# A transformer block on one core: sums, `den`, fills and weight loads of the tile loop in another order

## The chip, the core and the metric

The kernel runs on one core of a Trainium2 chip. The metric is the device time of one execution in microseconds (us); a time is given as the median of several runs. The five engines work side by side, each through its own list of instructions in order: PE (TensorE, matrix products), DVE (VectorE), ACT (ScalarE), POOL (GpSimd) and SP (SyncE, which here only issues DMAs). They wait for one another by semaphores.

## The reference

One sequence of 2048 tokens with 512 channels goes through two blocks, both with a residual sum:

```python
x = A_x
h = x + _A_ref(_layernorm(x), A_wqkv, A_w_phi, A_wo)
h2 = h + _B_ref(_layernorm(h), B_w1, B_b1, B_w2, B_b2)
```

`_A_ref` is linear attention with 32 heads of 16 channels. The queries and keys of each head go through a small matrix `w_phi` and two softmaxes, of the logits and of their negatives, side by side: `phi_q` and `phi_k`. With `kv = phi_k^T v` and `z` the sum of `phi_k` over all tokens, the output of a head is `phi_q kv / (phi_q z + 1e-6)`, and `wo` mixes the heads. `_B_ref` is an MLP across tokens: `w2 gelu(w1 layernorm(h)^T + b1) + b2`, with 2048 tokens in, 1792 hidden and 2048 out, shared over the channels. All is float32. Each large product is made of three products of the operands' high and low parts (`mm3`: high by high, high by low, low by high).

## The kernel before

The tokens are cut into `NT` = 16 tiles of 128. The work has four stages.

*Weights and K/V (to L415).* `w_phi` is folded into the query and key weights. Then, tile by tile, K logits (`k_logits`), V (`v_proj`) and the sums of `kv` are made; the products of K and V take turns on PE, in two PSUM banks each (`ps_k`, `ps_v`). In the turns t = 4, 6, 8, 9, 11 and 13 (`Q_AT`) one tile of queries goes along: its product (`q_mm`), its logits (`q_logits`: maximum, minimum and one or two subtractions on DVE), its exponential on ACT (`q_exp`) and the sums of its exponentials (`q_sums`, two reductions on DVE, one for each sign, L215). Here a scheduler of the framework decides how the instructions of PE, DVE, ACT and POOL interleave.

*Transition (L417 to L504).* From here the order on these four engines is the order of the program (a manual schedule); only SP's DMAs are still placed by the scheduler. Two last K tiles, the last V tiles, and `zB` (the sum of `phi_k`, spread over the partitions) are finished. `s_ez(t)` (L441, POOL) multiplies a tile's exponentials by `zB`. `s_den(t)` (L443, DVE, six steps) sums them (L454), combines them with the sums of exponentials and leaves `W[t]` (L462), the factor of each head. `s_pq(t)` (L465, POOL) multiplies the exponentials by `W[t]`. For tiles 0 and 1 `den` works in a PSUM tile of its own (`ps_d`, "dn"). `kvS` (L504, DVE) is `kv` times a mask.

*The loop over tiles (L658 to L697).* Round `it` works on several tiles at once. On PE, in this order: `s_num(it-1)` (L546, `pn`), the transposes `s_tr(it)` (L528, `tr`), in round 0 `s_kv` (L536, two transposes of `kvS`, which ACT copies to `kvB`), one item of `turn` (half a projection of queries, `q_half`, or a fill), `s_wo(it-1)` (`po`, twelve products), then the other items of `turn`. On ACT: the moments of `h(it-2)` (L577 to L579), `oh` (L550, the high part of `pn`), `pht` (L530, two copies of `tr`), an exponential, `hn` and its high part `hs` (L587, L57), and the high parts of MLP weights (`his`, L600). On DVE: logits, `ol` (L555, the low part of `pn`), the sums of a tile, `s_den(it+2)`, `s_h(it-1)` (L571, the residual sum `h`), and the low parts of weights (`flush`, L606). On POOL: `s_pq(it+1)`, `s_rstd(it-2)` (L582 and L583), `s_ez(it+3)`, the low part of `hs` (L58), and the logits' negatives (`negate`).

What ties a round to the one before: `pn` and `po` share one PSUM tile (`ps_n`, one buffer), so `s_num` waits until DVE has read `po` in `s_h`, and `po` until DVE has read `pn` in `ol`. `tr` and `den` share another (`ps_t`, one buffer), so the transposes of a round wait until `den` of the round before has left `W`, and `den` waits until ACT has read `tr`.

A fill is one tile's share of the first product of the MLP: `fill(p)` adds tile `FN[p]` to two PSUM banks of the pair `p` of hidden tiles (six matmuls). `LAG` = 4 lets `fill(0)` take tile `it - 4`; `fill(1)` begins once all logits are made (round 8), with up to two tiles in a round. `Q_TURNS` lists the halves of query projections of rounds 0 to 7. `fill_load` brings the weights of two tiles (one DMA of 256 KB), `his` and `flush` make their high and low parts, in four buffers each (`wf`). `turn` (L648) decides by `it`, `FL` and `FN` when to load.

*The MLP (from L711).* The remaining fills for `p` = 2 to 6, gelu, and the second product in a form with seven products for eight. Here the scheduler orders the instructions again.

Of the kernel before, what the change touches and what calls it, by code (L numbers as in the profile page):

```python
# [11 lines left out]
AF = mybir.ActivationFunctionType  # L12
# [7 lines left out]
NT = S // P  # L20
# [4 lines left out]
Q_AT = (4, 6, 8, 9, 11, 13)  # L25
V_NOT = (0, 1, 11)
Q_TURNS = ((0, 1), (0, 1), (0, 1), (0, 1), (0,), (1,), (0,), (1,))
LAG = 4
WARM = 9
EPS = 1e-5  # L30

# [2 lines left out]
def block_kernel(ctx: ExitStack, tc: tile.TileContext, x, xT, wT, phic, wo, w1, b1, w2, b2,  # L34
                 kvmask, ident_in, out):
    nc = tc.nc
# [12 lines left out]
    r2 = cst.tile([P, NT], F32, name="r2")  # L49
# [42 lines left out]
    ps_d = a1.enter_context(tc.tile_pool(name="ps_d", bufs=1, space=PSUM))  # L92
# [4 lines left out]
    def load_x(t):  # L97
        raw = kk.tile([P, KD, P], F32, name="xraw", bufs=3)
        nc.sync.dma_start(raw, xT[t])
        return raw  # L100

    def load_h(t):
        XH[t] = kk.tile([P, D], F32, name="xh", bufs=3)
        nc.sync.dma_start(XH[t], x[t * P:(t + 1) * P, :])

    def split_x(t, raw):
        X[t] = big.tile([P, 2, KD, P], F32R, name="xs", tag="big")
        split(X[t][:, 0], X[t][:, 1], raw, nc.gpsimd)
# [53 lines left out]
    def turns(*lists):  # L162

        return [ops[i] for i in range(max(map(len, lists))) for ops in lists if i < len(ops)]

    def run(*lists):
        for op in turns(*lists):
            op()
# [11 lines left out]
    def k_logits(t):  # L180
        k_ops(t, proj(t, wkh, wkl, ps_k, "pk_ps"))
        exps(t, PK[t])
# [8 lines left out]
    def k_norm(t, z=True):  # L191
        sk = wk.tile([P, 2 * H], F32, name="sk", bufs=2)
        nc.vector.reduce_sum(sk, heads(PK[t]), axis=AX.X)
        nc.vector.reciprocal(sk, sk)  # L194
        nc.gpsimd.tensor_mul(heads(PK[t]), heads(PK[t]), sk.unsqueeze(2).to_broadcast([P, 2 * H, DH]))  # L195
        if z and t == 0:
            nc.gpsimd.tensor_copy(zacc, PK[t])
        elif z:
            nc.gpsimd.tensor_add(zacc, zacc, PK[t])  # L199

    def kv(t):

        for n in range(4):
            for c in range(4):
                g = n // 2 * 4 + c
                j = 2 * g + n % 2
                nc.tensor.matmul(kvp[32 * c:32 * c + 32, n, :], VS[t][:, 32 * j:32 * j + 32],  # L207
                                 PK[t][:, g, n % 2 * 64:n % 2 * 64 + 64], start=(t == 0 and n == 0),
                                 stop=(t == NT - 1), skip_group_check=True)

    def q_sum(t):

        SQ[t] = sums[:, t]
        e = signs(EQ[t])
        return [lambda c=c: nc.vector.reduce_sum(SQ[t][:, :, 1 - c], e[:, :, c], axis=AX.X) for c in range(2)]  # L215
# [142 lines left out]
    q = {"mm": 0, "logits": 0, "exp": 0, "sum": 0}  # L358

    def q_mm():  # L360
        if q["mm"] < NT:
            PS[q["mm"]] = proj(q["mm"], wqh, wql, ps_q, "pu")
            q["mm"] += 1
# [9 lines left out]
    def q_exp(lag):  # L373
        n = q["exp"]
        if n < min(NT, q["logits"] - len(MN) - lag):
            exps(n, EQ[n])
            q["exp"] += 1

    def q_sums(lag):
        n = q["sum"]  # L380
        if n < min(NT, q["exp"] - lag + NT * (q["exp"] == NT)):
            q["sum"] += 1
            return q_sum(n)
        return []

    def v_kv():

        nonlocal v
        v_proj(v)
        if v % 2 == 0:  # L390
            kv(v - 2)
            kv(v - 1)
        v += 1
# [4 lines left out]
    for t in range(3, NT - 1):  # L398
        if t + 2 < NT:
            raw = load_x(t + 2)  # L400
            load_h(t + 2)
        if t > 3:
            k_logits(t)
        if t > 3 and t not in V_NOT:
            v_kv()
        if t > 0:
            k_norm(t - 1)
        if t + 2 < NT:
            split_x(t + 2, raw)
            stats_x(t + 2)  # L410
        if t in Q_AT:
            q_mm()
            run(q_logits(0))
            q_exp(0)
            run(q_sums(1))  # L415

    ms = ExitStack()  # L417
    ms.enter_context(tc.manual_schedule(engines={ET.PE, ET.DVE, ET.Activation, ET.Pool}))
# [24 lines left out]
    def s_den(t, pool, name):  # L443


        W[t] = az.tile([P, NPR, 2, 2], F32, name="w", bufs=3)
        other = SQ[t]
        at = []

        def first():  # L450
            bank = pool.tile([P, 8, P], F32, name=name)[:, 0] if name == "tr" else pool.tile([P, P], F32, name=name)
            at.extend((bank[:, 0:64].rearrange("p (g c h) -> p g c h", c=2, h=2),
                       bank[:, 64:96].rearrange("p (g h) -> p g h", h=2)))
            nc.vector.reduce_sum(at[0].rearrange("p g c h -> p (g c h)"), heads(EZ[t]), axis=AX.X)  # L454

        return [first,
                lambda: nc.vector.scalar_tensor_tensor(at[0][:, :, 0], other[:, :, 1], 1e-6, at[0][:, :, 0],
                                                       op0=ALU.mult, op1=ALU.add),
                lambda: nc.vector.tensor_mul(at[0], other, at[0]),
                lambda: nc.vector.reduce_sum(at[1], at[0].rearrange("p g c h -> p g h c"), axis=AX.X),  # L460
                lambda: nc.vector.reciprocal(at[1], at[1]),
                lambda: nc.vector.tensor_mul(W[t], other, at[1].unsqueeze(2).to_broadcast([P, NPR, 2, 2]))]  # L462
# [38 lines left out]
    q_mm()  # L501
    kv(NT - 2)
    kv(NT - 1)
    nc.vector.tensor_mul(kvS, kvp, mask.unsqueeze(1).to_broadcast([P, 4, 64]))  # L504


# [6 lines left out]
    ps_t = a2.enter_context(tc.tile_pool(name="ps_t", bufs=1, space=PSUM, reuse_waits="tile"))  # L513
    ps_n = a2.enter_context(tc.tile_pool(name="ps_n", bufs=1, space=PSUM, reuse_waits="tile"))
    HN, HT, PHT, OS, PO, VE = {}, {}, {}, {}, {}, {}
# [16 lines left out]
    def s_kv():  # L532

        pt = banks("pt")[:, 0, 0:2]
        for b in range(2):
            nc.tensor.transpose(pt[:, b, :], kvS[:, 2 * b:2 * b + 2, :].rearrange("p n f -> p (n f)"), ident)  # L536
        nc.scalar.activation(kvB, pt, AF.Copy)
# [15 lines left out]
    def s_ol(t):  # L553
        oh, ol, pn = OS[t]
        return [lambda: nc.vector.tensor_sub(ol, pn, oh)]  # L555
# [24 lines left out]

    def s_rstd(t):
        nc.gpsimd.tensor_tensor(r2[:, t:t + 1], VE[t][:, 0:1], mhalf[:, :1], op=ALU.pow)  # L582
        nc.gpsimd.tensor_mul(VE[t][:, 1:2], VE[t][:, 1:2], r2[:, t:t + 1])  # L583

    def s_hn(t):
        hn = ak.tile([P, D], F32, name="hn")
        nc.scalar.activation(hn, HT[t], AF.Identity, scale=r2[:, t:t + 1], bias=VE[t][:, 1:2])  # L587
        HN[t] = big.tile([P, 2, D], F32R, name="hs", tag="big")
        split(HN[t][:, 0], HN[t][:, 1], hn, nc.gpsimd)
# [6 lines left out]
    def his():  # L596
        while COMING:
            LATER.append(COMING.pop(0))
            _, raw, wh_ = LATER[-1]
            nc.scalar.activation(wh_, raw, AF.Copy)  # L600
# [17 lines left out]
    FN, FL = [0] * (NF // 2), [0] * (NF // 2)  # L618
# [29 lines left out]
    def turn(it):  # L648

        halves = Q_TURNS[it] if it < len(Q_TURNS) else ()  # L650
        n = [FN[0] <= it - LAG and FN[0] < NT, min(2, max(0, it - LAG + 1 - FN[1])) if q["logits"] == NT else 0]
        for p in range(2):
            if it >= LAG - 2 + 2 * p and FL[p] < min(NT, FN[p] + n[p] + 1 + p):
                fill_load(p)
        return ([lambda i=i: q_half(i) for i in halves] + [lambda: fill(0, ps_f)] * n[0]
                + [lambda: fill(1, ps_q)] * n[1])

    for it in range(NT + 3):  # L658
        if it < NT:
            s_x(it)  # L660
        shifted = q["logits"] - len(MN)
        ql = q_logits(0)
        work = turn(it)
        if 0 <= it - 2 < NT:
            s_moments(it - 2)
        if 0 <= it - 1 < NT:
            s_num(it - 1)
        if it < NT:
            s_tr(it)
        if it == 0:  # L670
            s_kv()
        if it + 1 < NT:
            s_pq(it + 1)
        for w in work[:1]:
            w()
        if q["exp"] < shifted:
            q_exp(0)
        if 0 <= it - 2 < NT:
            s_rstd(it - 2)
        if it + 3 < NT:  # L680
            s_ez(it + 3)
        if 0 <= it - 2 < NT:
            s_hn(it - 2)
        negate()
        his()
        sm = q_sums(0) if q["sum"] <= it + 3 else []
        run(ql[:2] + (s_ol(it - 1) if 0 <= it - 1 < NT else []) + ql[2:] + sm[:1])
        run(s_den(it + 2, ps_t, "tr") if it + 2 < NT else [])
        run(sm[1:])
        if 0 <= it - 1 < NT:  # L690
            s_wo(it - 1)
        for w in work[1:]:
            w()
        if 0 <= it - 1 < NT:
            s_h(it - 1)
        flush()
# [104 lines left out]
    for n, (sp, p) in enumerate(STEPS):  # L801
        t = 2 * sp
# [93 lines left out]
```

## Time and profile before

| what | value |
|---|---|
| median of 3 runs | 531.26 us (531.11 to 532.04) |
| the profiled execution | 532.08 us, its span 530.3 us |
| PE clock granted | 0.999 of full speed |
| rounds 0 to 18 of the loop over tiles | from about 143 to 270 us of the span |

The span reaches from the first to the last instruction of the profiled execution; its device time lies a little around it. Times within the span count from its start. A line number in a profile is that of the kernel before, unless it is said otherwise. In a timeline row stand the start, the duration, the engine, the line, the operation, "out<-in", the shapes, the count, and in square brackets how long the engine had been idle and what it then waited for. In a row of groups stand the count, the summed busy time in us, the mean of one in ns, and the idle time ahead. A row of the waits names who waited for whom, the microseconds in total, how often, and the longest. PEld is the loading of weights into PE, which goes beside its products.

### The profile page before, as it was taken

The numbers are of one execution on the slowest core, as the hardware profiler recorded it, in microseconds if no ns is written. First come the engines' busy times: TensorE is split into PE (matmuls) and PEld (weight loads), VectorE is DVE, ScalarE is ACT, GpSimd is POOL, SyncE is SP. The second block draws the span as 40 slices with busy tenths as digits, with TensorE's granted clock in tenths as the row PEclk, the third lists the DMA queues.
The fourth block names the chain that finished last, engine by engine and source line by source line (L and its number), as shares of the span: only waits on it lengthen the run. The fifth ranks groups of instructions, "written<-read, shape, count | busy, mean of one in ns | idle before, by whom it ended". The sixth has DMA issues, their size and how long they took to land.

```text
span 530.3 us, 10156 instructions
## 1 busy us (share of the span) xinstructions
PE 520.0 (98%) x4000; PEld 447.1 (84%) x4000; DVE 381.6 (72%) x680; ACT 272.6 (51%) x460; POOL 231.5 (44%) x190
## 2 busy tenths in 40 slices
PE   8999999999999999999999999999999999999996
PEld 7888888887877777777778888888899999999996
DVE  6893999976889988685235424835758877978774
ACT  6998834525256768666664423525453342342330
POOL 2479699876989999985333000000001101101110
PEclk9999999999999999999999999999999999999999
DMA  8644210013303323433255333543014555545631
GB/s 310 185 132 120 82 40 21 1 40 102 101 21 99 102 80 102 138 101 101 80 160 178 99 101 99 160 114 86 20 41 107 140 152 135 129 134 123 158 79 41
DMA packets 45487, 55.85 MB, mean 105 GB/s; under 512 B 3968, under 2 KB 33024, under 8 KB 45440
## 3 DMA queue, kind: packets, MB, share of 16 engines
q1 hardware_dynamic: 43136, 51.38, 30.9%
q0 software_dynamic: 2016, 3.67, 5.1%
q8 instruction: 31, 0.51, 0.4%
q10 hardware_dynamic: 288, 0.17, 0.1%
q14 instruction: 16, 0.13, 0.1%
HBM read 46.81 MB, written 8.39 MB: 104 GB/s over the span
## 4 chain that ended last, share of the span: by engine, by line
PE 87%; DVE 6%; ACT 4%; issue 2%; POOL 1%; DVEq 0%; ACTq 0%; POOLq 0%
PE py L790 26%; PE pu L62 11%; PE pu L63 11%; PE pu L64 11%; PE pv L63 3%; PE pv L64 3%; PE pv L62 3%; PE pk_ps L62 2%; PE pk_ps L64 2%; PE pk_ps L63 2%; PE po L64 2%; PE po L62 2%; PE po L63 2%; PE kvp L207 2%; PE tr L528 1%
## 5 line engine op out<-in xcount | busy, mean ns | idle before, releaser
L828 POOL DMA_DIRECT2D out<-ot x14 | 12.5, 1001 | 216.1 <-DVE ot L826 216.1
L790 PE MATMUL py<-uf,whi 128*128 128x256 f32 x560 | 96.2, 283 | 0.0
L62 PE MATMUL pu<-hs,whi 128*128 128x512 f32 x224 | 88.4, 394 | 1.1 <-ACT whi L600 1.1
L57 ACT ACTIVATE whi<-wraw 128x1792 fp32r<-128x1792 f32 x28 | 47.7, 1704 | 77.9 <-PE py L790 72.5
L63 PE MATMUL pu<-hs,whi 128*128 128x512 f32 x224 | 87.3, 390 | 0.0
L64 PE MATMUL pu<-hs,wlo 128*128 128x512 f32 x224 | 86.9, 389 | 0.0
L790 PEld LDWEIGHTS py<-uf,whi 128*128 128x128 f32 x560 | 83.3, 192 | 0.0
L606 DVE TENSOR_TENSOR wlo<-wraw,whi 128x512 fp32r<-128x512 f32 x56 | 44.2, 796 | 49.7 <-ACT whi L600 49.5
L790 PE MATMUL py<-uf,wlo 128*128 128x256 f32 x280 | 69.9, 283 | 0.0
L58 DVE TENSOR_TENSOR wlo<-wraw,whi 128x1792 fp32r<-128x1792 f32 x28 | 56.6, 2022 | 16.2 <-ACT whi L57 15.7
L600 ACT ACTIVATE whi<-wraw 128x512 fp32r<-128x512 f32 x56 | 34.6, 625 | 47.9 <-PE pu L63 43.7
L62 PEld LDWEIGHTS pu<-hs,whi 128*128 128x128 f32 x224 | 42.0, 188 | 10.9 <-ACT whi L600 1.8
L790 PEld LDWEIGHTS py<-uf,wlo 128*128 128x128 f32 x280 | 49.7, 192 | 0.0
L64 PEld LDWEIGHTS pu<-hs,wlo 128*128 128x128 f32 x224 | 42.0, 188 | 8.8
L63 PEld LDWEIGHTS pu<-hs,whi 128*128 128x128 f32 x224 | 42.1, 188 | 8.4
L441 POOL TENSOR_TENSOR ez<-eq,zB 128x1024 f32<-128x1024 f32 x16 | 38.5, 2409 | 3.9 <-ACT zB L485 3.9
L790 PE MATMUL py<-un,whi 128*128 128x256 f32 x224 | 38.4, 283 | 0.0
L195 POOL TENSOR_TENSOR pk<-pk,sk 128x1024 f32<-128x1024 f32 x16 | 31.0, 1942 | 9.9 <-DVE sk L194 9.2
L465 POOL TENSOR_TENSOR eq<-eq,w 128x1024 f32<-128x1024 f32 x16 | 32.8, 2052 | 1.7 <-DVE w L462 1.4
L790 PEld LDWEIGHTS py<-un,whi 128*128 128x128 f32 x224 | 33.2, 192 | 0.1
L199 POOL TENSOR_TENSOR zacc<-zacc,pk 128x1024 f32<-128x1024 f32 x13 | 31.3, 2405 | 0.5
L790 PE MATMUL py<-un,wlo 128*128 128x256 f32 x112 | 27.6, 283 | 0.0
(171 smaller groups left out, 1165.3 us busy)
## 6 DMA issues: line engine op xcount, KB each, us to landing
wraw<-in_w SPq DMA_DIRECT2D x112, 256.0 KB, 2.8
xraw<-in_xT SPq DMA_DIRECT2D x16, 256.0 KB, 3.1
xh<-in_x SPq DMA_DIRECT2D x16, 256.0 KB, 2.7
h<-in_x SPq DMA_DIRECT2D x16, 256.0 KB, 2.6
out<-h SPq DMA_DIRECT2D x16, 256.0 KB, 2.0
out<-ot POOLq DMA_DIRECT2D x14, 256.0 KB, 4.3
wraw<-in_wT SPq DMA_DIRECT2D x12, 256.0 KB, 5.1
wo<-in_wo SPq DMA_DIRECT2D x4, 256.0 KB, 4.2
```

What stands on the lines that cost most here:

```text
L57: nc.scalar.activation(hi, src, AF.Copy)
L58: lo_engine.tensor_sub(lo, src, hi)
L62: nc.tensor.matmul(o, ah, bh, start=first, stop=False)
L63: nc.tensor.matmul(o, ah, bl, start=False, stop=False)
L64: nc.tensor.matmul(o, al, bh, start=False, stop=last)
L195: nc.gpsimd.tensor_mul(heads(PK[t]), heads(PK[t]), sk.unsqueeze(2).to_broadcast([P, 2 * H, DH]))
L199: nc.gpsimd.tensor_add(zacc, zacc, PK[t])
L441: nc.gpsimd.tensor_mul(EZ[t], EQ[t], zB)
L465: nc.gpsimd.tensor_mul(heads(EQ[t]), heads(EQ[t]), W[t].rearrange("p g c h -> p (g c h)").unsqueeze(2).to_broadcast([P, 2 * H, DH]))
L600: nc.scalar.activation(wh_, raw, AF.Copy)
L606: LO.append(nc.vector.tensor_sub(wl_, raw, wh_).ins)
L790: nc.tensor.matmul(o, a[x], b[:, y], start=start and i == 0, stop=stop and i == 2, skip_group_check=True)
```

## The change

Six edits, all in the order of the work; what is computed stays the same.

- The sums of a query tile in the K/V stage no longer lag one tile behind (`q_sums(0)`). In the loop, a tile's sums are made in round 0 and then only when `q["sum"] <= it + 2`; with logits in the round both reductions stand ahead of `den`, otherwise one ahead of `ol` and one behind it.
- `s_den(2)` moves from round 0 to the transition, ahead of `kvS`, and works in the "dn" tile; round 0 has no `den`.
- `s_kv` moves behind the first item of `turn` in round 0.
- The product of the mean and `r` (L583) moves from POOL to ACT, ahead of `hn`.
- `LAG` becomes 3: fills take tile `it - 3`, and the loop ends one round earlier (`NT + 2`). The loads of `p = 1` begin in round 7, those of `p = 0` in round 2 as before; in round 16 loads may go two tiles further ahead.
- In rounds after 16 the high parts of weights are made ahead of the moments.

```diff
-LAG = 4
+LAG = 3
...
             q_exp(0)
-            run(q_sums(1))
+            run(q_sums(0))
...
     kv(NT - 1)
+    run(s_den(2, ps_d, "dn"))
     nc.vector.tensor_mul(kvS, kvp, mask.unsqueeze(1).to_broadcast([P, 4, 64]))
...
     def s_rstd(t):
         nc.gpsimd.tensor_tensor(r2[:, t:t + 1], VE[t][:, 0:1], mhalf[:, :1], op=ALU.pow)
-        nc.gpsimd.tensor_mul(VE[t][:, 1:2], VE[t][:, 1:2], r2[:, t:t + 1])
 
     def s_hn(t):
         hn = ak.tile([P, D], F32, name="hn")
+        nc.scalar.activation(VE[t][:, 1:2], VE[t][:, 1:2], AF.Copy, scale=r2[:, t:t + 1])
         nc.scalar.activation(hn, HT[t], AF.Identity, scale=r2[:, t:t + 1], bias=VE[t][:, 1:2])
...
-            if it >= LAG - 2 + 2 * p and FL[p] < min(NT, FN[p] + n[p] + 1 + p):
+            ahead = n[p] + 1 + p + 2 * (it == NT)
+            if it >= (LAG - 1, len(Q_TURNS) - 1)[p] and FL[p] < min(NT, FN[p] + ahead):
                 fill_load(p)
...
-    for it in range(NT + 3):
+    for it in range(NT + 2):
...
         work = turn(it)
+        if it > NT:
+            his()
...
-        if it == 0:
-            s_kv()
         if it + 1 < NT:
             s_pq(it + 1)
         for w in work[:1]:
             w()
+        if it == 0:
+            s_kv()
...
-        sm = q_sums(0) if q["sum"] <= it + 3 else []
-        run(ql[:2] + (s_ol(it - 1) if 0 <= it - 1 < NT else []) + ql[2:] + sm[:1])
-        run(s_den(it + 2, ps_t, "tr") if it + 2 < NT else [])
-        run(sm[1:])
+        sm = q_sums(0) if it == 0 or q["sum"] <= it + 2 else []
+        ol = s_ol(it - 1) if 0 <= it - 1 < NT else []
+        run(ql[:2] + ol + ql[2:] + sm if ql else sm[:1] + ol + sm[1:])
+        if it > 0 and it + 2 < NT:
+            run(s_den(it + 2, ps_t, "tr"))
```

## The prediction

> **What bounds the kernel now.** I read the page first, then who waited for whom on the tensor engine, then busy time in stretches cut where each round's `s_num` starts, then the chain of waits inside one slow round.
>
> ```profile
> span 530.3 us, 10156 instructions
> ```
>
> ```profile
> PE 520.0 (98%) x4000; PEld 447.1 (84%) x4000; DVE 381.6 (72%) x680; ACT 272.6 (51%) x460; POOL 231.5 (44%) x190
> ```
>
> ```profile
> PE pn L546 <- DVE h L571: 2.1, 4, 0.7
> ...
> PE tr L528 <- DVE w L462: 0.6, 1, 0.6
> ```
>
> The tensor engine (PE) is busy for 98% of the span, and the change takes no matrix product away. So the only thing to win is PE's idle time, and these two rows name most of it: 2.1 us in which `s_num` waited for the residual sum `h`, and 0.6 us in which a transpose waited for the weights `W`. Where these lie (window; PE, PEld, DVE, ACT, POOL busy; clock; DMA):
>
> ```profile
> 154.48:161.70 7.22, 6.97 (x74) 5.43 (x74) 6.90 (x15) 5.41 (x11) 6.48 (x7) 1.00 0.26 75
> 161.70:169.47 7.77, 7.11 (x72) 5.35 (x73) 7.60 (x16) 5.14 (x11) 7.61 (x8) 1.00 0.31 101
> 169.47:177.03 7.56, 6.98 (x72) 5.43 (x73) 6.66 (x15) 5.67 (x12) 7.40 (x8) 1.00 0.23 72
> 177.03:184.00 6.97, 6.97 (x72) 5.42 (x73) 6.29 (x13) 5.79 (x12) 6.89 (x6) 1.00 0.36 116
> 184.00:191.93 7.93, 7.28 (x73) 5.35 (x73) 7.62 (x15) 5.25 (x11) 7.77 (x8) 1.00 0.31 98
> ...
> 259.70:270.00 10.30, 9.27 (x69) 6.98 (x68) 2.08 (x5) 6.57 (x15) 3.19 (x6) 1.00 0.32 102
> 270.00:385.00 115.00, 114.92 (x508) 95.05 (x509) 59.41 (x112) 50.00 (x90) 7.76 (x9) 1.00 0.38 113
> ```
>
> Rounds 2 to 6 of the loop over tiles, then the loop's end, then the MLP. Round 5 shows what a round costs when PE never waits: 6.97 us. Rounds 2, 3, 4 and 6 take 0.25, 0.80, 0.59 and 0.96 more: idle of 0.25, 0.66, 0.58 and 0.65, and a slower pace of 0.14 in round 3 and 0.31 in round 6. After 270 PE is full again, so whatever is won before 270 reaches the end. Why a round is long, from the chain of waits:
>
> ```profile
> 169.59 0.82 ACT hj L578 x2
> ...
> 172.54 0.59 DVE smq L215
> 173.14 1.14 DVE tr L454
> ...
> 176.20 0.70 DVE h L571 x2
> ```
>
> It is a ring: `h` lets ScalarE (ACT) take the moments, ACT's order puts `oh` behind them, VectorE (DVE) needs `oh` for `ol`, then works through shift, sums (L215) and `den` (its first reduction is L454) to the next `h`, which frees the bank for `s_num`. From the moments' second step (169.59) to the end of the next `h` (176.20 + 0.62) it is 7.23 us; with the first step of 0.20 (its row stands below) and the hand-over from `h` to ACT the ring is some 7.5 us, more than PE's 6.97. That DVE shows idle time in these rounds is no contradiction: it waits for `oh` while ACT does the moments, and both are links of the same ring.
>
> **The change, part by part.**
>
> *Sums (L415, L686).* By the order of the built program, no sums stand in rounds 1 to 4; tile 5's pair moves to the K/V stage, tile 6's to round 0, and tiles 7 to 15 follow one round later than before (rounds 5 to 13), ahead of `den`.
>
> ```profile
> L215 DVE TENSOR_REDUCE smq<-eq 128x32 f32<-128x512 f32 x32 | 21.2, 674 | 0.2 <-ACT eq L171 0.2
> ```
>
> A sum lasts 0.67 us, of which the next instruction overlaps a little: it advances DVE by 0.60 (172.54 to 173.14), a pair by 1.2. In rounds 2, 3 and 4 the ring shrinks from some 7.5 to 6.3, under 6.97: their idle (0.25, 0.66, 0.58) goes, with about 0.6 to spare. What is late next there is PE itself. In round 5 there are no logits, so one sum runs in the gap in which DVE waits for `oh`, and the ring stays under 6.97. Round 6 keeps logits and both sums ahead of `den`; no weight part precedes it now, and round 5 leaves it the lead of about 0.6, so of its 0.65 I let 0.2 stand. Saved: 0.25 + 0.66 + 0.58 + 0.45 = 1.94. Of the slower pace (0.14 + 0.31 = 0.45), matmuls that started one by one behind late operands, I take half, 0.25; bounds 0 and 0.45.
>
> *The third tile's `den` ahead of `kvS`; `s_kv` behind the first half projection.*
>
> ```profile
> 139.20 2.40 POOL L441 TENSOR_TENSOR ez<-eq,zB 128x1024 f32<-128x1024 f32 x1
> ```
>
> ```profile
> 143.26 0.42 DVE L504 TENSOR_TENSOR kvS<-kvp,mask 128x256 f32<-128x256 f32 x1 [1.31 <-PE kvp L207]
> ```
>
> ```profile
> 145.40 1.22 DVE L454 TENSOR_REDUCE tr<-ez 128x64 f32<-128x1024 f32 x1
> ...
> 147.81 0.22 DVE L462 TENSOR_TENSOR w<-smq,tr 128x64 f32<-128x64 f32 x1
> ```
>
> ```profile
> 148.18 0.71 PE L528 MATMUL tr<-ident,eq 64*128 64x64 f32 x16 [0.60 <-DVE w L462]
> ```
>
> DVE is idle from 141.95 (143.26 less 1.31). Tile 2's `ez` is ready at 141.60, so `den(2)` starts at 141.95 and ends after 2.63 us (145.40 to 148.03) at 144.58, 3.4 earlier. It also uses another PSUM tile, so round 1's transposes don't wait: 0.60 saved. Queued behind it on DVE is `kvS`, on which `s_kv`, `kvB` and the first `s_num` hang; `kvS` slips to about 145.0. The stretch from 270 shows the pace of a full PE, 115.00 us for 508 matmuls or 0.227 each, so the half projection of six that now stands ahead of `s_kv` takes 1.37. PE ends `kvp` at about 143.2, transposes for 0.7 and reaches `s_kv` at about 145.2, cover 0.2; without it PE would wait at most 1.2. After 144.58 DVE has `kvS` (0.4), three steps of logits (1.8), the pair of sums (1.2), two steps of the next logits (1.2) and `ol(0)` (0.6), so `ol(0)` ends at 149.8. PE, its transposes now at 147.58, wants it 0.7 + 1.37 later, at 149.6: I charge 0.2.
>
> *`VE*r` on ACT.*
>
> ```profile
> L577 ACT ACTIVATE ve<-ve 128x1 f32<-128x1 f32 x16 | 3.2, 203 | 28.2 <-DVE h L571 28.2
> ```
>
> ```profile
> L583 POOL TENSOR_TENSOR ve<-ve,r 128x1 f32<-128x1 f32 x16 | 3.1, 192 | 1.2
> ```
>
> The first row is an ACT operation of the new one's shape, the second the POOL operation that goes. POOL loses 0.19, ACT gains 0.20 per tile. ACT is busy 5.1 to 5.8 us in these rounds and it stands behind `oh` and `pht`; it waits for POOL's `r` just as `hn` did, with `hn`, `hs` and the weights' high parts queued behind it, so it only makes the fills' operand some 0.2 later. Cost nothing, hidden by the slack worked out under the first rival.
>
> *Fills three behind, weight loads at other times.* PE gets no more work: one fill of 1.37 goes into round 3, the loop loses its last round. `p = 1` loads from round 7 instead of 4, `p = 0` in even rounds. Each load is a DMA on SP's queue, which stands in the built order several `h` loads ahead of its conversion; the ACT and DVE conversions number four in rounds 2 to 7 as before. Zero here.
>
> *The last weights.* Before, `p = 0`'s last pair came in round 17 and was converted behind tile 15's `hs`:
>
> ```profile
> 269.41 1.66 ACT L600 ACTIVATE whi<-wraw 128x512 fp32r<-128x512 f32 x3
> ```
>
> ```profile
> 270.08 0.50 PE L62 MATMUL pu<-hs,whi 128*128 128x512 f32 x1 [1.11 <-ACT whi L600]
> ```
>
> ```profile
> 264.98 0.69 DVE L571 SCALAR_TENSOR_TENSOR h<-po,h 128x512 f32<-128x512 f32 x1 [3.18 <-PE po L64]
> ```
>
> ```profile
> 269.58 1.28 POOL L58 TENSOR_TENSOR hs<-hn,hs 128x512 fp32r<-128x512 f32 x1 [1.59 <-ACT hs L57]
> ```
>
> With a lag of 3 the parity puts that load in round 16, converted behind tile 14's `hs`, some 6 us earlier than 269.4: the 1.06 (1.03 by the window, 1.11 by the row) goes. What is late next is tile 15's operand: 5.9 us from its `h` to 270.86. The built order puts 42 matmuls, 9.6 us, between `po(15)` and the first use of it (tile 13's half, tile 14 and four tiles of `p = 2`), so it is covered by over 3 us.
>
> Sum: 0.60 - 0.20 + 1.94 + 0.25 + 1.06 = **3.65 us saved**. The profiled execution took 532.08 around its span of 530.3, so by its own time 528.4; the median of the three runs is 531.26, which gives **527.6**.
>
> **Rivals.**
>
> *POOL takes over.* POOL is as busy as DVE in these rounds, and its low parts now have one round less before a fill wants them.
>
> ```profile
> 148.11 1.94 POOL L465 TENSOR_TENSOR eq<-eq,w 128x1024 f32<-128x1024 f32 x1 [0.91 <-DVE w L462]
> ...
> 177.72 2.39 POOL L465 TENSOR_TENSOR eq<-eq,w 128x1024 f32<-128x1024 f32 x1
> ```
>
> ```profile
> 197.56 1.30 POOL L58 TENSOR_TENSOR hs<-hn,hs 128x512 fp32r<-128x512 f32 x1
> ```
>
> ```profile
> 200.14 0.50 PE L62 MATMUL pu<-hs,whi 128*128 128x512 f32 x1
> ```
>
> ```profile
> 176.81 1.50 DVE L606 TENSOR_TENSOR wlo<-wraw,whi 128x512 fp32r<-128x512 f32 x1
> ```
>
> Tile 5's low part ends at 198.86; round 8's first fill, which will want tile 5, stood at 200.14: 1.3 of slack. PE comes 2.6 earlier, less 1.37 for the extra fill; POOL gains the 0.91 for which it waits for `W(2)`, and 0.19 in each of five rounds: slack 1.3 - 1.2 + 1.9 = 2.0. It decides if POOL is more than 2.0 late, for example because `eq` takes 2.39 instead of 1.94 in every round up to there, 3.2 in all: then some 1.2 to 1.5 of the gain is lost, 529.1.
> The Trainium skill (SBUF — State Buffer, Who interferes with whom) says that a VectorE instruction with two SBUF inputs and a GpSimd one that reads SBUF exclude each other fully, and that reductions never do. By that rule the moved sums cost POOL nothing, and only the four `wlo` do; the trace agrees in kind (1.50 beside 2.39), though both were stretched, neither blocked for the other's length.
>
> *Slower: sums crowd the K logits.* Without the lag of one, a turn's sums wait for that turn's own exponential and stand ahead of K's logits in DVE's order. If K's banks then came free too late, each of the six turns would cost PE a pair, 1.2 us: 7.2 - 3.65, so 534.8. It decides once a bank's slack is under 1.2; here it is 4.9 (the bank of the `K` read last at 88.28 is wanted at 93.22):
>
> ```profile
> 87.61 0.67 DVE L149 TENSOR_TENSOR pk<-mn,pk_ps 128x512 f32<-128x512 f32 x1
> ```
>
> ```profile
> 93.22 0.39 PE L62 MATMUL pk_ps<-wkh,xs 128*128 128x512 f32 x1
> ```
>
> *It doesn't do what it says.* The early `his()` finds nothing to convert in round 17, since no load is left by then; if the load of round 16 lands late, only the 1.06 is missing: 528.7.
>
> **Chances.** Forecast 0.70 (own range 526.9 to 528.4), POOL 0.10 (529.1), last weights 0.07 (528.7), gains cancelled by something unseen 0.05 (531), K logits 0.08 (534.8). Faster by over 0.2%, about what a measurement of this kernel tells from no change: 0.87; within: 0.05; slower: 0.08. The range goes from all idle and all slow pace removed (2.1 + 0.6 + 1.1 + 0.45 = 4.25, with half a microsecond for spread) to the POOL case with a little more: 526.5 to 529.6.
>
> **What would show it.** Right: `pn <- h` falls from 2.1 to about 0.2, `tr <- w` and `pu <- whi` vanish, rounds 2 to 7 take 6.97 each (8.34 in round 3), and 270 on stays full. Wrong: fills that wait for `hs` (POOL), `pt` or `po` that waits for DVE in round 0 or 1 by over 0.4, idle PE between 60 and 143, or waits for `whi` after the loop.

## The result and the profile after

| | median (runs) | lowest to highest |
|---|---|---|
| before | 531.61 us (4) | 531.11 to 532.04 |
| after | 528.53 us (4) | 527.96 to 529.15 |

The ratio after / before is 0.9943, with a 95% interval of 0.9925 to 0.9960: 3.1 us less, or 0.57%. The forecast was 527.6, with its own range of 526.9 to 528.4 and a whole range to 529.6. It started from a median of 531.26 for the kernel before; from 531.61 the same 3.65 saved would give 528.0, so 0.35 of the miss of 0.9 is the starting point. Two executions far off all the others, one of the kernel before (1032.76 us) and one of b_sums (1805.23 us), are left out of the ratios. The profiled execution of the changed kernel took 528.31 us (span 526.5).

The page of the changed kernel, busy time by engine:

```profile
PE 518.9 (99%) x4000; PEld 446.6 (85%) x4000; DVE 386.2 (73%) x680; ACT 278.2 (53%) x476; POOL 229.1 (44%) x174
```

Who waited for whom on PE, in the changed kernel (total, times, longest). Its line numbers are up to 5 above those of before: L547 is `pn`, L556 `ol`, L572 `h`, L607 `wlo`.

```profile
PE po L62 <- DVE ol L556: 1.0, 1, 1.0
...
PE pn L547 <- DVE h L572: 0.2, 1, 0.2
```

`tr <- w` and `pu <- whi` are gone, and `pn <- h` fell from 2.1 to 0.2, as forecast. The first row is new. Rounds 2 to 6 of the changed kernel, cut as those of before:

```profile
153.46:160.35 6.89, 6.89 (x73) 5.39 (x72) 6.20 (x13) 6.07 (x13) 5.40 (x5) 1.00 0.26 78
160.35:168.64 8.29, 8.29 (x79) 6.53 (x78) 7.02 (x15) 6.50 (x14) 8.13 (x8) 1.00 0.39 128
168.64:175.54 6.90, 6.90 (x73) 5.40 (x72) 4.95 (x12) 5.34 (x10) 6.90 (x6) 1.00 0.10 38
175.54:182.47 6.93, 6.93 (x74) 5.40 (x73) 5.74 (x14) 5.68 (x12) 6.85 (x6) 1.00 0.33 111
182.47:189.65 7.18, 6.97 (x73) 5.43 (x73) 6.25 (x15) 5.82 (x12) 7.10 (x7) 1.00 0.20 56
```

PE is full in all but the last, where 0.21 is left of 0.65. Round 3 (8.29) holds one more fill, as announced. Now both kernels over longer stretches: rounds 0 and 1, rounds 2 to 6, rounds 7 to 15, and from there to the first product of the second MLP layer. Before:

```profile
143.12:154.48 11.36, 10.76 (x109) 8.35 (x103) 10.07 (x22) 4.51 (x9) 10.30 (x9) 1.00 0.17 58
154.48:191.93 37.45, 35.31 (x361) 26.97 (x361) 35.06 (x70) 27.26 (x53) 36.16 (x33) 1.00 0.29 92
191.93:259.68 67.75, 67.75 (x672) 53.14 (x673) 47.25 (x95) 46.51 (x96) 53.10 (x46) 1.00 0.33 103
259.68:270.04 10.36, 9.29 (x69) 7.00 (x68) 2.10 (x5) 6.63 (x15) 3.23 (x6) 1.00 0.31 101
270.04:384.58 114.54, 114.50 (x504) 94.63 (x505) 59.23 (x111) 49.54 (x88) 7.72 (x9) 1.00 0.38 113
```

After:

```profile
142.61:153.46 10.85, 10.85 (x110) 8.25 (x103) 9.98 (x23) 4.61 (x9) 10.67 (x9) 1.00 0.20 63
153.46:189.65 36.19, 35.98 (x367) 28.15 (x367) 30.16 (x64) 29.40 (x58) 34.39 (x28) 1.00 0.26 84
189.65:260.13 70.48, 69.44 (x679) 54.07 (x679) 55.95 (x99) 49.98 (x106) 52.50 (x37) 1.00 0.34 108
260.13:268.00 7.87, 7.87 (x64) 6.13 (x64) 2.90 (x7) 5.88 (x14) 1.84 (x2) 1.00 0.31 102
268.00:380.80 112.80, 112.80 (x499) 93.39 (x498) 57.12 (x109) 50.19 (x89) 8.70 (x10) 1.00 0.39 115
```

One fill (1.37) moved into the second stretch and one into the third, out of the last two. With that taken out, the four parts gain 0.51, 2.63 (37.45 - 36.19 + 1.37), -1.36 (67.75 - 70.48 + 1.37) and 1.49 (124.90 - 120.67 - 2.74): 3.27 in all, of which 2.60 is idle time and 0.67 is pace. I call the length from the first transpose of the loop to the first product of the second layer the **loop length**: 241.46 before, 238.19 after. It is the measure for the experiments, because the rest of the 3.8 us between the two profiled executions, 0.51, lies elsewhere, at the very start:

```profile
10.70 2.13 PE L124 MATMUL pk_ps<-wkh,xs 128*128 128x512 f32 x8 [0.80 <-ACT wkh L279]
```

```profile
10.17 2.13 PE L124 MATMUL pk_ps<-wkh,xs 128*128 128x512 f32 x8 [0.80 <-ACT wkh L279]
```

The first K product begins 0.53 earlier in the execution after (second row) than in the one before, in code that the diff does not touch: ACT takes up the second block of weights at 6.32 instead of 6.60, and where the rest of the 0.53 comes from was not traced. In the twelve kernels below this start lies anywhere from 9.94 to 11.09, and from it to the first transpose it is 132.4 or 132.5 us in every one: so much for the K/V stage, which the sums do not disturb at all.

**Where 1.04 us was lost.** DVE and POOL of the changed kernel at the turn from round 8 to round 9, then PE:

```profile
203.50 0.68 DVE L572 SCALAR_TENSOR_TENSOR h<-po,h 128x512 f32<-128x512 f32 x1
...
204.11 3.53 DVE L607 TENSOR_TENSOR wlo<-wraw,whi 128x512 fp32r<-128x512 f32 x2
207.57 0.67 DVE L215 TENSOR_REDUCE smq<-eq 128x32 f32<-128x512 f32 x1
208.16 0.68 DVE L556 TENSOR_TENSOR ol<-pn,oh 128x512 fp32r<-128x512 f32 x1
```

```profile
203.45 1.30 POOL L58 TENSOR_TENSOR hs<-hn,hs 128x512 fp32r<-128x512 f32 x1
204.71 2.39 POOL L465 TENSOR_TENSOR eq<-eq,w 128x1024 f32<-128x1024 f32 x1
207.06 1.00 POOL L583 TENSOR_TENSOR r<-ve,mhalf 128x1 f32<-128x1 f32 x1
```

```profile
208.90 0.50 PE L62 MATMUL po<-woh,oh 128*128 128x512 f32 x1 [1.04 <-DVE ol L556]
```

Both `p = 0` and `p = 1` load in round 8, so two low parts follow `h(7)`. They last 3.53 us instead of some 1.3. POOL's rows tell why, if the two engines cannot read at once: the first part waits for the end of `hs` (204.75), runs for 0.45, and `eq`, 1.94 elsewhere, is held up by just that (2.39). The second part waits for the end of `eq` (207.10) and holds up `r` by 0.45 (1.00 instead of 0.55). Then a sum stands ahead of `ol`, for another 0.60, and `po(8)` waits.

### The profile page after: what moved, and what is told of

The parts are those of the page before. It is cut to its first block, busy times and chain, and to the rows that moved or that the text cites. A ratio compares the mean times of both kernels' runs of the same rounds, so it can differ in the third digit from the quotient of the medians.

```text
span 526.5 us, 10155 instructions
## 1 busy us (share of the span) xinstructions
PE 518.9 (99%) x4000; PEld 446.6 (85%) x4000; DVE 386.2 (73%) x680; ACT 278.2 (53%) x476; POOL 229.1 (44%) x174
## 4 chain that ended last, share of the span: by engine, by line
PE 95%; DVE 3%; ACT 1%; issue 0%; DVEq 0%
PE py L795 26%; PE pu L62 13%; PE pu L63 12%; PE pu L64 12%; PE pv L63 3%; PE pv L64 3%; PE po L62 3%; PE pv L62 3%; PE po L64 3%; PE po L63 3%; PE pk_ps L62 2%; PE pk_ps L64 2%; PE pk_ps L63 2%; PE pn L547 2%; PE tr L529 2%; PE kvp L207 2%
## 5 line engine op out<-in xcount | busy, mean ns | idle before, releaser
L607 DVE TENSOR_TENSOR wlo<-wraw,whi 128x512 fp32r<-128x512 f32 x56 | 48.5, 872 | 44.6 <-ACT whi L601 44.4
L58 POOL TENSOR_TENSOR hs<-hn,hs 128x512 fp32r<-128x512 f32 x16 | 20.7, 1293 | 17.9 <-ACT hs L57 17.9
```

Source lines behind the costliest of these rows:

```text
L58: lo_engine.tensor_sub(lo, src, hi)
L607: LO.append(nc.vector.tensor_sub(wl_, raw, wh_).ins)
```

## The experiments

All but two start from the changed kernel. The loop length is from each one's profiled execution, the ratio from timed runs beside the kernel before. The intervals of u_sums, b_lag, u_kv, fix_ol, fix_load, u_pow and best overlap that of the change, so by time alone they can't be told from it; how they differ from it is read from the loop length and the rows of one trace each.

**Put back the sums (u_sums).**

```diff
-            run(q_sums(0))
+            run(q_sums(1))
...
-        sm = q_sums(0) if it == 0 or q["sum"] <= it + 2 else []
-        ol = s_ol(it - 1) if 0 <= it - 1 < NT else []
-        run(ql[:2] + ol + ql[2:] + sm if ql else sm[:1] + ol + sm[1:])
+        sm = q_sums(0) if q["sum"] <= it + 3 else []
+        run(ql[:2] + (s_ol(it - 1) if 0 <= it - 1 < NT else []) + ql[2:] + sm[:1])
...
             run(s_den(it + 2, ps_t, "tr"))
+        run(sm[1:])
```

> The changed kernel with the sums alone put back: the lag of one in the K/V stage, tile 5's pair in round 0 and so on one round earlier, one reduction ahead of den and one behind it. Theory A (the sums made the ring of h, moments, oh, ol, den too long): PE's waits of pn for h come back in rounds 2, 3, 4 and 6, from 0.2 to about 2.1 us; the 1.04 us in which po(8) waited for ol shrinks to about 0.4, because ol stands ahead of the sums again; time 528.5 + 1.9 + 0.4 - 0.6, about 530.2. Rival (the ring became short for another reason, the earlier den(2) or the third fill in round 3): pn waits for h stay under 0.5 us and the time stays within 0.5 of 528.5.

Measured: 528.65 us, ratio 0.9944 (0.9929 to 0.9959), the same as the change itself; loop length 238.37, 0.18 more.

```profile
PE pn L547 <- DVE h L572: 1.0, 3, 0.5
...
PE po L62 <- DVE ol L556: 0.2, 1, 0.2
```

The time is the rival's, the waits are neither side's. Those for `h` come back only by half, 0.22, 0.21 and 0.55 at the ends of rounds 2, 4 and 6 and none in round 3, and against them stands the 1.04 of `po(8)`, which goes altogether. So my theory that the sums carried the gain fell: among the other edits they are worth 0.2 us. `ol(8)` is not earlier, though:

```profile
208.67 0.68 DVE L556 TENSOR_TENSOR ol<-pn,oh 128x512 fp32r<-128x512 f32 x1
```

```profile
209.41 0.50 PE L62 MATMUL po<-woh,oh 128*128 128x512 f32 x1
```

Counted from the first transpose of the loop (142.91 here, 142.61 in the changed kernel), `ol(8)` ends at 66.44 here and at 66.23 there, and `po(8)` starts at 66.50 and at 66.29. It is PE that comes later here: in the changed kernel it stood ready 1.04 earlier, at 65.25. So up to that point the sums bring PE 1.25 us forward, and the wait for `ol` takes 1.04 of it back. No run puts the sums back where that wait is gone.

**Put back the fills and loads (u_lag).**

```diff
-LAG = 3
+LAG = 4
...
-            ahead = n[p] + 1 + p + 2 * (it == NT)
-            if it >= (LAG - 1, len(Q_TURNS) - 1)[p] and FL[p] < min(NT, FN[p] + ahead):
+            if it >= LAG - 2 + 2 * p and FL[p] < min(NT, FN[p] + n[p] + 1 + p):
...
-    for it in range(NT + 2):
+    for it in range(NT + 3):
...
-        if it > NT:
-            his()
```

> The changed kernel with the fills four tiles behind, the weight loads at the rounds of the kernel before and no early high parts. Theory A (the 1.04 us of po(8) came from two weight loads in round 8, whose low parts took 3.53 us of DVE ahead of ol): the wait of po(8) goes, since p = 1 then starts in round 4 and only one load falls in round 8; the wait of pu for whi in the last round comes back with 1.1 us; time 528.5 - 1.04 + 1.1, about 528.6, with up to 0.6 more where round 3 loses its fill. Rival B (it is the sum ahead of ol alone): po(8) still waits 0.6 or more, and the time is about 529.5.

Measured: 530.79 us, ratio 0.9983 (0.9973 to 0.9992); loop length 240.66, 2.47 more.

```profile
PE po L62 <- DVE ol L556: 1.2, 1, 1.2
PE pu L62 <- ACT whi L601: 1.2, 1, 1.2
...
PE pn L547 <- DVE h L572: 0.7, 1, 0.7
```

The wait of `po(8)` went and that for `whi` came back, as theory A had it; the time is 1.6 us above the most it allowed. The first row is another one: `po(5)`, at 185.65, followed by 0.66 at the end of round 6. ACT, then DVE, ahead of it:

```profile
179.68 0.29 ACT L587 ACTIVATE ve<-ve,r 128x1 f32<-128x1 f32 x1 [1.26 <-POOL r L583]
```

```profile
182.04 1.76 DVE L607 TENSOR_TENSOR wlo<-wraw,whi 128x512 fp32r<-128x512 f32 x1 [1.06 <-ACT whi L601]
```

POOL is late with `r`, ACT waits 1.26 for it with the high part of a weight behind, and DVE waits 1.06 for that. I read it so: with fills four behind round 3 has no fill and lasts 6.9 us, in which POOL, with some 6.9 us of its own, catches nothing up; the fill in round 3 gives POOL and DVE 1.4 us in which PE works. This run puts back two things at once, though, the fills and a low part in round 5. fix_load below parts them: it has low parts in rounds 2, 4 and 5 as this run has, but keeps the fill in round 3, and there `pn` waits the same 0.66 and `po(5)` not at all. So the 0.66 goes with the low part in round 5, and the 1.23 with the missing fill.

**Each of the two alone, on the kernel before (b_lag, b_sums).** First the fills and loads:

```diff
-LAG = 4
+LAG = 3
...
-            if it >= LAG - 2 + 2 * p and FL[p] < min(NT, FN[p] + n[p] + 1 + p):
+            ahead = n[p] + 1 + p + 2 * (it == NT)
+            if it >= (LAG - 1, len(Q_TURNS) - 1)[p] and FL[p] < min(NT, FN[p] + ahead):
...
-    for it in range(NT + 3):
+    for it in range(NT + 2):
...
+        if it > NT:
+            his()
```

> The kernel before with only the fills three behind, the loads of the change and the early high parts. Prediction's terms: only the 1.06 us of the last weights, so 530.5. Theory formed after the run with the sums put back: the fill that moves into round 3 gives POOL and DVE 1.4 us there in which PE works, so most waits of pn for h go as well (2.1 to about 1.0); time 531.6 - 1.1 - 1.1, about 529.4.

Measured: 529.10 us, ratio 0.9955 (0.9943 to 0.9968); loop length 239.19, 2.27 less than before. Its waits:

```profile
PE pn L546 <- DVE h L571: 1.1, 3, 0.6
...
PE tr L528 <- DVE w L462: 0.6, 1, 0.6
PE po L62 <- DVE ol L555: 0.5, 1, 0.5
```

As the later theory had it: `pn <- h` falls from 2.1 to 1.1 with no sum moved. It is the fill that does it and not the loads: up to round 4 the low parts stand in the same rounds as before (2 and 4), and just there the wait at the end of round 3 goes from 0.66 to nothing and that at the end of round 4 from 0.58 to 0.21. Round 6, ahead of which a low part goes as well, keeps 0.59 of 0.66. Then the sums, with `den(2)` left in round 0:

```diff
-            run(q_sums(1))
+            run(q_sums(0))
...
-        sm = q_sums(0) if q["sum"] <= it + 3 else []
-        run(ql[:2] + (s_ol(it - 1) if 0 <= it - 1 < NT else []) + ql[2:] + sm[:1])
+        sm = q_sums(0) if it == 0 or q["sum"] <= it + 2 else []
+        ol = s_ol(it - 1) if 0 <= it - 1 < NT else []
+        run(ql[:2] + ol + ql[2:] + sm if ql else sm[:1] + ol + sm[1:])
...
-        run(sm[1:])
```

> The kernel before with only the sums edit (no lag in the K/V stage, later in the loop, both ahead of den with logits). Prediction's terms: 1.94 + 0.25 us saved, less 1.1 because round 0's pair now stands ahead of den(2), so about 530.5. Theory formed after the other runs: with fills four behind the rounds stay at 7 us, in which POOL is full, and waits of po(5) for ol (1.2) and of pn(6) for h (0.7) take the place of those removed, tr waits 1.7 instead of 0.6, whi stays at 1.1; idle 4.7 against 3.85 before, so 531.6 + 0.5 to 0.9, about 532.3: by itself this edit gains nothing.

Measured: 532.91 us, ratio 1.0016 (1.0006 to 1.0026); loop length 241.10, 0.36 less. Its waits:

```profile
PE tr L528 <- DVE w L462: 1.8, 1, 1.8
PE pu L62 <- ACT whi L600: 1.1, 1, 1.1
...
PE pn L546 <- DVE h L571: 0.6, 1, 0.6
PE po L62 <- DVE ol L555: 0.5, 1, 0.5
```

The idle of the loop is 4.0, against 3.85 before and 4.7 as the later theory had it: of the waits for `h` only the 0.64 at the end of round 6 is left, and waits of another kind have taken the place of the others, 1.2 of them because the pair of sums in round 0 stands ahead of `den(2)`. The time is longer than the loop says; the last section has a likely reason. Alone the sums gain nothing in time.

**Put back `den(2)` (u_den), put back `s_kv` (u_kv).**

```diff
-    run(s_den(2, ps_d, "dn"))
...
-        if it > 0 and it + 2 < NT:
+        if it + 2 < NT:
             run(s_den(it + 2, ps_t, "tr"))
```

> The changed kernel with den(2) alone put back into round 0, in the tr tile, behind the logits and the pair of sums. Theory A: DVE then reaches den(2) after kvS (142.7), three steps of logits (1.8) and the pair of sums (1.2), W(2) is there at about 148.7, and round 1's transposes, wanted at about 147.0, wait for it some 1.7 us, more than the 0.6 of the kernel before; time 528.5 + 1.7, about 530.2. Rival (the wait is 0.6 as before, so that the sums in round 0 cost nothing there): 529.1. Rival 2 (den(2) in the transition only pushes kvS, and putting it back costs nothing): 528.5.

Measured: 530.23 us, ratio 0.9982 (0.9970 to 0.9994); loop length 241.36.

```profile
148.75 0.87 PE L528 MATMUL tr<-ident,eq 64*128 64x64 f32 x16 [1.73 <-DVE w L462]
```

The wait is 1.73, as theory A worked it out. So this edit is what pays for the pair of sums in round 0. The loop is 3.2 longer rather than 1.7; the rest is PE's clock (last section).

```diff
+        if it == 0:
+            s_kv()
         if it + 1 < NT:
             s_pq(it + 1)
         for w in work[:1]:
             w()
-        if it == 0:
-            s_kv()
```

> The changed kernel with s_kv back ahead of the first half projection of round 0. The prediction: without that cover PE waits at most 1.2 us. In the trace of the changed kernel kvS ends at 144.33 and PE would reach s_kv at 143.25, so theory A: PE waits about 1.1 us for kvS, time about 529.6. Rival (kvB on ACT, not kvS, is what the first s_num needs, and it has room): the wait is only moved and the time stays at 528.5.

Measured: 529.38 us, ratio 0.9955 (0.9940 to 0.9969); loop length 239.12, 0.93 more.

```profile
144.35 0.44 PE L537 MATMUL pt<-ident,kvS 128*128 128x128 f32 x2 [1.05 <-DVE kvS L505]
```

Theory A: the half projection ahead of `s_kv` hides 1.05 us.

**The lost 1.04: `ol` first (fix_ol), other rounds for the loads (fix_load), POOL's operation left out (no_pq).**

```diff
-        run(ql[:2] + ol + ql[2:] + sm if ql else sm[:1] + ol + sm[1:])
+        run(ql[:2] + ol + ql[2:] + sm if ql else ol + sm if it > 8 else sm[:1] + ol + sm[1:])
```

> The changed kernel with ol ahead of both sums in rounds 9 to 13 (before: one sum ahead of ol), nothing else. Theory A (two stretched low parts AND the sum stood ahead of ol): the sum is 0.60 of the 1.04 us, so po(8) still waits about 0.4 us; time about 527.9. Rival B (the sum ahead of ol is all of it): no wait is left, time about 527.3. Rival C (den, now 0.6 later behind both sums, makes the next h late): new waits of pn for h in rounds 10 to 13, time 528.5 or more.

Measured: 528.13 us, ratio 0.9933 (0.9918 to 0.9948); loop length 237.60, 0.59 less.

```profile
PE po L62 <- DVE ol L556: 0.4, 1, 0.4
```

0.4 of the 1.04 is left (0.45 in its row of the timeline): theory A. b_lag says the same from the other side: it has the two loads and not the sum ahead of `ol`, and its `po(8)` waits 0.47.

```diff
-            if it >= (LAG - 1, len(Q_TURNS) - 1)[p] and FL[p] < min(NT, FN[p] + ahead):
+            ahead += 2 * (p == 1 and it == 7)
+            if it >= (LAG - 1, 5)[p] and (p, it) != (1, 8) and FL[p] < min(NT, FN[p] + ahead):
```

> The changed kernel with the second load of p = 1 in round 7 and its first in round 5, none in round 8, so that one low part instead of two follows h in round 8; the order of sums and ol is untouched. Theory A (two loads in one round): DVE is 1.7 us earlier at ol(8), po(8) doesn't wait, time about 527.3. Rival B (the sum ahead of ol alone): po(8) still waits some 0.6 us, time about 528.1. Rival C (the parts moved to rounds 5 and 7 lengthen the ring there): pn waits for h in rounds 6 and 8 grow from 0.2 to 0.7 or more, time 528.5.

Measured: 528.09 us, ratio 0.9932 (0.9917 to 0.9947); loop length 237.52, 0.67 less.

```profile
PE pn L547 <- DVE h L572: 0.7, 1, 0.7
```

No wait of `po` is left, with the sum still ahead of `ol`: rival B falls, and theory A has the wait right. Its time of 527.3 isn't reached, because rival C is right for round 6: the part that moved to round 5 raises the wait at its end from 0.21 to 0.66. At the end of round 8, where C had another one, there is none. So both the two loads and the sum are needed for the 1.04: without the sum 0.45 of it is left, without the second load nothing.

```diff
-        if it + 1 < NT:
+        if it + 1 < NT and it != 9:
             s_pq(it + 1)
```

> The changed kernel without the multiplication of tile 10's exponentials by W on POOL in round 9 (the work is left out, one POOL operation of 2.4 us). It asks whether POOL is what stretches the two low parts on DVE at 204 (3.53 us for two, 0.69 each elsewhere). Theory A: without it the two take 1.4 to 2.2 us, po(8) doesn't wait, time about 527.3. Rival B (ez and the low part of hs on POOL, which then stand there instead, stretch them as much, or the stretch has another cause): they take 3 us or more, po(8) waits as before, time 528.5.

Measured: 527.07 us, ratio 0.9911 (0.9898 to 0.9925); loop length 236.86; no wait of `po`. The two parts:

```profile
203.87 1.77 DVE L607 TENSOR_TENSOR wlo<-wraw,whi 128x512 fp32r<-128x512 f32 x2
```

1.77 instead of 3.53 with one POOL operation less: theory A. It is POOL that makes them long.

**POOL's room: `VE*r` back on POOL (u_pow), a tiny power more in rounds 2 to 7 (pool_x).**

```diff
         nc.gpsimd.tensor_tensor(r2[:, t:t + 1], VE[t][:, 0:1], mhalf[:, :1], op=ALU.pow)
+        nc.gpsimd.tensor_mul(VE[t][:, 1:2], VE[t][:, 1:2], r2[:, t:t + 1])
...
-        nc.scalar.activation(VE[t][:, 1:2], VE[t][:, 1:2], AF.Copy, scale=r2[:, t:t + 1])
```

> The changed kernel with the product of mean and r back on POOL. The prediction: worth nothing. In the trace of the changed kernel POOL has no idle time from 160 to 197 and the low part of tile 5 ends 0.9 us ahead of the first fill of round 8 (196.91 against 197.82). Theory A: five products of 0.19 make POOL 0.95 later there, just about the slack, so PE waits 0 to 0.2 us, time 528.5 to 528.7. Rival (POOL is the bound, the rival of the prediction): PE waits 0.5 us or more for hs, time 529.1 or more.

Measured: 528.27 us, ratio 0.9933 (0.9918 to 0.9948); loop length 237.91, 0.28 less. PE doesn't wait for `hs`, and the 1.04 of `po(8)` is gone; in its place `po(10)` waits 0.33. DVE, then POOL, at the same turn:

```profile
204.50 2.52 DVE L607 TENSOR_TENSOR wlo<-wraw,whi 128x512 fp32r<-128x512 f32 x2 [0.51 <-ACT whi L601]
```

```profile
204.74 1.74 POOL L58 TENSOR_TENSOR hs<-hn,hs 128x512 fp32r<-128x512 f32 x1
206.44 2.38 POOL L465 TENSOR_TENSOR eq<-eq,w 128x1024 f32<-128x1024 f32 x1
```

None had foreseen this. DVE now starts 0.24 ahead of `hs` instead of behind it, so the first part runs at once and `hs` is held up by 0.45 (1.74 instead of 1.28); the second waits for `hs` alone. Who is first decides over a microsecond.

```diff
             s_ez(it + 3)
+        if 2 <= it < 8:
+            pj = ak.tile([P, 1], F32, name="pj", bufs=1)
+            nc.gpsimd.tensor_tensor(pj, VE[it - 2][:, 0:1], mhalf[:, :1], op=ALU.pow)
```

> The changed kernel with one more tiny power on POOL in each of rounds 2 to 7 (0.55 us each, its result unused), behind ez. It measures how much room POOL has. Theory A (slack 0.9 us at the first fill of round 8): by round 8 POOL is some 2.7 us later, so PE waits for hs there in sum 1.5 to 2.2 us, and the time is 530.0 to 530.7. Rival (POOL has the 2.0 us of slack that the prediction worked out): waits of 0.5 to 1.0, time 529.0 to 529.5. Rival 2 (POOL is far from mattering): no wait, 528.5.

Measured: 530.44 us, ratio 0.9979 (0.9967 to 0.9991); loop length 239.98, 1.79 more. PE, DVE and POOL:

```profile
PE po L62 <- DVE ol L556: 2.2, 2, 1.8
```

```profile
205.52 4.13 DVE L607 TENSOR_TENSOR wlo<-wraw,whi 128x512 fp32r<-128x512 f32 x2 [0.54 <-ACT whi L601]
```

```profile
205.45 1.30 POOL L58 TENSOR_TENSOR hs<-hn,hs 128x512 fp32r<-128x512 f32 x1
206.69 2.40 POOL L465 TENSOR_TENSOR eq<-eq,w 128x1024 f32<-128x1024 f32 x1
```

The price is theory A's, the place is not: PE waits for `ol`, not for `hs`. DVE came 0.07 behind the start of `hs` and waited for all of it, then for all of `eq`: 1.23 + 0.45 + 1.94 + 0.5 = 4.1.

**All together (best).** fix_load, fix_ol, and tile 7's sums in round 4, where DVE waits 1.4 us for `oh`:

```diff
-        sm = q_sums(0) if it == 0 or q["sum"] <= it + 2 else []
+        sm = q_sums(0) if it == 0 or q["sum"] <= it + 2 + (it in (4, 5)) else []
...
-        run(ql[:2] + ol + ql[2:] + sm if ql else sm[:1] + ol + sm[1:])
+        run(ql[:2] + sm + ol + ql[2:] if it == 4 else ql[:2] + ol + ql[2:] + sm if ql else ol + sm if it > 8 else sm[:1] + ol + sm[1:])
```

> The changed kernel with three edits: the loads of p = 1 in rounds 5 and 7 and none in round 8; ol ahead of both sums from round 9 on; tile 7's sums in round 4 in the gap ahead of ol, tile 8's in round 5, none in round 6. From the earlier runs: the wait of po(8) goes with the loads (seen), and the 0.66 us in which pn waited for h at round 7 goes because round 6 then has no sums, 1.2 us less. Theory: no wait of PE in the tile loop of 0.2 us or more, from the first transpose to the first py 236.6 to 237.0 us instead of 238.2, time 527.0. Rival (DVE's room is used up: each edit moves the wait to the next round): a wait of 0.4 us or more in rounds 4 to 8, time 527.8 or more.

Measured: 528.00 us, ratio 0.9930 (0.9918 to 0.9943); loop length 237.24. The view of the waits lists two rows, both from the first eleven microseconds:

```profile
PE pk_ps L287 <- DVE eps L53: 1.1, 1, 1.1
PE pk_ps L124 <- ACT wkh L279: 0.8, 1, 0.8
```

The waits went as the theory had it; the time did not, 528.0 where it had 527.0 and the rival 527.8 or more. The loop is 0.95 shorter than that of the change, less than the 1.2 to 1.6 expected and less than the 1.25 of idle that is gone; the gain over the change, 0.5 us by the medians, is inside both intervals, so by time alone it isn't shown. This profiled execution had a late start, its first K product at 10.82.

## Why the prediction was right, and where its steps were not

- *`tr <- w`, 0.60 saved:* right. *`po(0)`, 0.20 charged:* nothing was lost; `kvS` ended at 144.33 where I had 145.0 (0.5 of it by the early start), and PE waited neither for it nor for `ol(0)`. u_den and u_kv bear out the working: without the one edit PE waits 1.73, without the other 1.05.
- *Sums, 1.94 saved in rounds 2 to 6:* 2.14 of idle became 0.21, the size of the forecast. For rounds 2 to 4 the ring as I worked it out holds: in b_sums and u_lag, with the sums moved and the fills four behind, no wait for `h` is left there. But in both the wait comes back in round 6, where `po(5)` waits 0.48 and 1.23. **"Fills three behind, weight loads at other times ... Zero here" is what failed.** I counted the fill in round 3 as work moved, not as 1.37 us in which DVE and POOL catch up while PE is busy. It keeps `po(5)` from waiting, and with no sum moved at all it takes away the wait at the end of round 3 and most of that of round 4 (b_lag). The end of round 6 needs both the sums and the load moved out of round 5, which I had booked under the sums ("no weight part precedes it now"): without the sums 0.55 and 0.59 are left (u_sums, b_lag), without the load's move 0.66 (u_lag, fix_load). So that the size came out is partly luck: the sums were credited with what the fills and loads gave.
- *Pace, 0.25 taken:* 0.70 in rounds 2 to 6, above my bound of 0.45. A full round took 6.90 in the changed kernel where I read 6.97 from before.
- *Loads at other times, zero:* also wrong, on the other side: round 8's two loads cost 1.04 of idle, together with the sum ahead of `ol`. In the same stretch 0.32 of pace was lost, whose cause is not shown. I had asked whether each load lands in time and whether as many conversions remain in rounds 2 to 7, but not what stands behind the conversions on DVE in round 9, where the sums edit had just put a reduction ahead of `ol`.
- *`VE*r` on ACT, zero:* undone, the loop is 0.28 shorter (0.57 less idle, 0.29 more busy time on PE), too little for the timed runs to show. What changes the idle time is the moment at which POOL and DVE meet.
- *Last weights, 1.06 saved:* right (1.11), and tile 15's operand was covered.
- *Rivals:* K's logits were not crowded; the K/V stage kept its 132.4 us. POOL didn't take over through late fills, as I had put it, but POOL is close: pool_x shows it acting through `wlo` and `ol`. The last weights came in time: no wait for `whi` is left.

By the four stretches the forecast was 0.40, 2.19, 0 and 1.06 us saved; found were 0.51, 2.63, -1.36 and 1.49. Three were too small and one missed a loss, so 3.65 and 3.27 (3.1 in the medians) lie closer than their terms. That too is luck.

The prediction's sentence on the Trainium skill (SBUF — State Buffer, Who interferes with whom) has to be taken back in part. I wrote that both sides were stretched and neither blocked for the other's length. The rule says that the one that starts first holds the port for its whole instruction, and the rows above agree: each POOL operation that meets a `wlo` is longer by 0.45 (1.94 to 2.39, 1.28 to 1.74, 0.55 to 1.00), and each `wlo` is longer by what was left of the POOL operation. The waiting stands inside the durations, which is why I took it for a slower pace.

## What to carry to other kernels

Work that moves on the bound engine is not free of effect because it is the same work: where it goes, the other engines get time, and where it leaves, they lose it; so list their idle time round by round in the new order too. An edit that was meant to relieve a ring can be worth next to nothing beside another that relieves the same ring, or because the engine it frees runs into the next wait: undo each part alone and do each part alone (undone, the sums were worth 0.2 us of the loop and the fills and loads 2.5; alone, 0.4 and 2.3; some 1.1 of the latter is the wait for the last weights, which was forecast). Measure small edits from a landmark in the trace, where a start that varies by a microsecond doesn't blur them.

## What was not expected of the hardware

*DVE and POOL by turns.* The same pair of low parts took 1.77, 2.52, 3.53 or 4.13 us, by what POOL had started just before, and the profile counts the waiting as busy time on both engines.

*PE's clock after a wait.* In u_den's profiled execution, the stretches behind the wait of 1.73 us:

```profile
148.75:152.00 3.25, 3.25 (x22) 2.65 (x23) 3.25 (x5) 2.12 (x3) 3.25 (x2) 0.56 0.00 0
152.00:156.60 4.60, 4.60 (x21) 3.51 (x19) 2.07 (x8) 0.43 (x2) 4.13 (x4) 0.94 0.00 0
```

The granted clock is 0.56 for 3.25 us, and a matmul of 512 columns then advances PE by 0.43 instead of 0.23. That costs some 1.4 us more than the wait itself. It isn't in every execution: u_den took 531.4 to 532.0 in the four with a mean clock of 0.995 or 0.996, and 529.7 to 530.3 in the six at 0.998 or more. b_sums waits 1.81 us, and its profiled execution, at a full clock, took 532.15; most of its others showed 0.995 to 0.997 and took 532.7 to 533.3, which would explain why its median lies above what its loop says. In pool_x (1.77) two of ten show a mean of 0.996 and take 532.0 to 532.1. The slow stretch itself is seen in u_den's trace alone, and there 0.67 us of small products (`s_num`) stand just ahead of the wait, so it isn't shown that the wait by itself is enough. Of the kernels whose longest wait in the loop was 1.23 or less, one execution of before shows a lower clock (0.948), and it was no longer than the others. The Trainium skill (TensorE: Matmul & The Clock Gate, HAM oscillation — how this bites in real kernels) gives gaps of over about 3.4 us as the ones to avoid; here the clock fell behind a gap of half that in some executions.
